# Reciprocals' transfers on ScalarE's queue, an earlier V, the last segment's skip in units 2 and 3, and a new rhythm of the convolution's lanes

## The chip, the core and the metric

The kernel runs on one core of a Trainium2 chip, as one program with one launch. The core has five engines with an instruction stream each: TensorE (PE, matmuls), VectorE (DVE), ScalarE (ACT), GpSimd (POOL) and SyncE (SP, which here does nothing but issue transfers). Transfers run on 16 DMA engines; SP, ACT and POOL can issue them, each on a queue of its own. The metric is the device time of one execution in microseconds, as the median of several runs.

## What is computed

A sequence of 2048 rows of 448 numbers goes through two branches, and a gate for each row mixes them. Branch A is a long convolution with a kernel that is itself computed from the parameters; branch B is attention in four segments of 512 rows with 16 heads of 28, causal inside a segment, plus a memory that later segments read from.

```python
# A: K = 2 Re sum_n C exp(A dt t); y = irfft(rfft(u) * rfft(K)); y + u * D_skip
# B, for each of the 4 segments s:
logits = einsum("bhqd,bhkd->bhqk", qs, ks) * scale + mask
a_dot = einsum("bhqk,bhkd->bhqd", softmax(logits), vs)
num, den = einsum("bhld,bhde->bhle", phi(qs), M), einsum("bhld,bhd->bhl", phi(qs), z) + 1e-6
o = g * num / den + (1 - g) * a_dot
M, z = M + phi(ks)^T vs, z + sum(phi(ks))
# out = gate * A + (1 - gate) * (o @ wo)
```

## The kernel before

The first half (up to about 430 us) builds the convolution's kernel, projects queries, keys and values and writes them to DRAM, and keeps the memory's part of each segment there too (`AM`, `DM`). The change lies in the second half, `second_half` (L1272).

Attention runs there in 16 **units**: unit `i` is one group of four heads (`hg = i % 4`) of segment `s = i // 4`. A unit has six **rounds**. In a round, `pair` (L1293) issues in turns the matmuls of the unit's logits (`weigh`, L1042: three parts into the PSUM bank `ps_w`, then ScalarE's Exp into `PT`) and the matmuls for the row maxima of the unit two ahead (`maxima`, L996: mask matmuls and products into the single bank `ps_mx`, then VectorE's reduction into `mx`). Behind that a round has one step each of other work, written as generators: in rounds 0 to 2 the weighted values of the unit before (`values`, L1074, into `ps_pv`, evicted to `pvs` by ScalarE), a step of the segment's end if one is open, and a step of the convolution. Matmuls keep their program order on TensorE (`k.mm`, L1463); what goes through `k.dve` and `k.sca` keeps it on VectorE and ScalarE (L1461). Transfers issued on SP may be reordered by the framework's planner when their data are ready earlier.

**The convolution** (`convolve`, L578) has 16 **lanes**, in units 1 to 12. A lane `m` is a transform T (`transform`, L610: eight matmuls on `gk` into the single bank `ps_c`, ScalarE's eviction to `ks`, and two transfers that swap the halves of `ks`), a product P (`product`, L618: eight matmuls on `gu` into `ps_c`, then two VectorE products with `ks` into `pr`, and the loads of a later lane), and a way back (`back`, L625) in two steps b and B of eight matmuls each into `ps_c`, with ScalarE's eviction to `bs` and a store to `BB` at the end. The loop (L645) gives one step at each `yield`: T of lane m, P of lane m - 1, then b and B of lane m - 2. The table `PACE` (L1402) says how many steps each round takes: 5.35 in a unit, so now and then a round has none.

**The end of a segment** (`seg_end`, L1190, opened in round 2 of units 4, 8 and 12) takes about 24 rounds. It loads four tiles `xt` of the input (`skip`, L1152), fetches the sums of the weights out of `pvs` into `dn` and the memory's sums into `dm`; `inverse` (L1097) takes reciprocals on VectorE, splits them into a high and a low part `rs` and sends both by transfer into the rows of `r8`, from where matmuls with `sel` spread them over the partitions. `norm` (L1131) does that for the softmax, `recall` (L1114) for the memory. Then follow the products with `wo` (`out_mm`), and `store` (L1165) adds the scaled `xt` and writes to `TB`. `scaled` (L1159) multiplies `xt` by the gate on ScalarE and by `D_skip` on GpSimd. All of these transfers go out on SP.

For the last segment the skip is done by itself (`skip_last`, L1171): four loads, four times `scaled`, four stores, in the last rounds of unit 10 and the first of unit 11; it shares the four `xt` buffers with `seg_end`. `values` asks for its segment's V (one buffer, 1 MB) at its first step, at the end of units 0, 4, 8 and 12.

Of the kernel before, what the change touches and what calls it, by code (L numbers as in the profile page):

```python
# [12 lines left out]
F32 = mybir.dt.float32  # L13
# [564 lines left out]
def convolve(nc, k, fp):  # L578

    NM = 16  # L580
    cf, cb, gk, gu, ks, pr = {}, {}, {}, {}, {}, {}
    rows = lambda t, m: t[4 * m : 4 * m + 4].rearrange("(i s) r n d -> (s r n) i d", i=2)
    halves = [slice(0, 64), slice(64, 128)]

    def load(m):
        if m >= NM:
            return
        if m % 2 == 0:
            cf[m // 2] = fp.tile([128, 4, 64], F32, tag="cf", name="cf", bufs=2)
            k.dma(cf[m // 2], k.c_fw[:, 2 * m : 2 * m + 4])  # L590
            cb[m // 2] = fp.tile([128, 2, 2, 2, 64], F32, tag="cb", name="cb", bufs=2)
            k.dma(cb[m // 2].rearrange("p m a s c -> p m (a s c)"), k.c_bk[:, m : m + 2])
        gk[m] = fp.tile([128, 2, D], F32, tag="gk", name="gk", bufs=2)
        k.dma(gk[m], rows(k.GK, m))
        gu[m] = fp.tile([128, 2, D], F32, tag="gu", name="gu", bufs=2)
        k.late(k.dma(gu[m], rows(k.GU, m)))

    def second(m, x):

        pt = k.ps("c")  # L600
        w = cf[m // 2]
        for s, r in enumerate(halves):
            for i, o in enumerate(halves):
                k.mm(
                    pt[o, s, :D], w[r, 2 * (m % 2) + i], x[r, i],
                    start=True, stop=True, tile_position=(64 * s, 64 * i),
                )
        return pt[:, :, :D]

    def transform(m):  # L610
        pt = second(m, gk.pop(m))
        ks[m] = fp.tile([128, 2, 2, D], F32, tag="ks", name="ks", bufs=2)
        k.sca.activation(ks[m][:, 0], pt, AF.Copy)
        x = ks[m].rearrange("(e a) b s d -> a e b s d", a=2)
        for a in range(2):
            k.dma(x[a, :, 1], x[1 - a, :, 0])

    def product(m):  # L618
        pt = second(m, gu.pop(m))
        pr[m] = fp.tile([128, 2, 2, D], F32, tag="pr", name="pr", bufs=2)  # L620
        x = ks.pop(m)
        for b in range(2):
            k.dve.tensor_tensor(pr[m][:, b], pt, x[:, b], ALU.mult)

    def back(m):  # L625

        pt = k.ps("c")
        w, x = cb[m // 2][:, m % 2], pr.pop(m)
        for b in range(2):
            if b:  # L630
                yield
            for i, r in enumerate(halves):
                for s, o in enumerate(halves):
                    k.mm(
                        pt[o, i, :D], w[r, b, s], x[r, b, s],
                        start=(b == 0), stop=(b == 1), tile_position=(64 * i, 64 * s),
                    )
        bs = fp.tile([128, 2, D], F32, tag="bs", name="bs", bufs=2)
        k.sca.activation(bs, pt[:, :, :D], AF.Copy)
        k.dma(k.BB[4 * m : 4 * m + 4].rearrange("(i s) r n d -> (s r n) i d", i=2), bs)  # L640

    load(0)
    load(1)
    yield
    for m in range(NM + 2):  # L645
        if m < NM:
            transform(m)
            yield
        if 1 <= m <= NM:
            product(m - 1)  # L650
            load(m + 1)
            yield
        if m >= 2:
            yield from back(m - 2)
            yield


def finish(nc, k, fp):
# [300 lines left out]
def attend(nc, k, ap):  # L959
# [82 lines left out]
    def weigh(i):  # L1042
# [23 lines left out]
        for hp in range(2):  # L1066
            for sl, pat in (
# [3 lines left out]
            ):  # L1071
                nc.gpsimd.affine_select(sl, sl, pat, ALU.is_ge, 0.0, base=0, channel_multiplier=-1)  # L1072

    def values(i):  # L1074
        s, hg = divmod(i, 4)
        if hg == 0:
            Vs[s] = ap.tile([128, 4, SEG], F32, tag="V", name="V", bufs=1)
            k.dma(Vs[s], k.VD[SEG * s : SEG * s + SEG].rearrange("(t p) h e -> p t (h e)", p=128))
            pvss[s] = ap.tile([128, 4, SEG], F32, tag="pvs", name="pvs", bufs=2)
        yield  # L1080
        V, pvs, PT = Vs[s], pvss[s], W.pop(i)
        pv = k.ps("pv")
        for kt in range(4):
            if kt in (1, 2):
                yield
            o = (0, 512, 1024, 896)[kt]
            for h in range(4):
                k.mm(
                    pv[32 * h : 32 * h + 32, 128 * kt :],
                    V[:, kt, (4 * hg + h) * 32 : (4 * hg + h) * 32 + 32],  # L1090
                    PT[:, h, o : o + SEG - 128 * kt],
                    start=(kt == 0), stop=(kt == 3), tile_position=(0, 32 * h),
                )
        act(pvs[:, hg], pv, AF.Copy)
        yield

    def inverse(x, rows, dst):  # L1097


        rc = ap.tile([128, 64], F32, tag="rc", name="rc", bufs=2)  # L1100
        rs = ap.tile([128, 2, 64], F32R, tag="rs", name="rs", bufs=2)
        v.reciprocal(rc, x)
        v.tensor_copy(rs[:, 0], rc)
        v.tensor_tensor(rs[:, 1], rc, rs[:, 0], ALU.subtract)
        for b in range(2):
            o = rows + 4 * b
            k.dma(
                dst[o : o + 4].rearrange("o h (i f) -> o (h i) f", f=64).bitcast(F32),
                rs[:, b].bitcast(F32),
            )  # L1110

    am, r8 = {}, {}

    def recall(s):  # L1114

        dn = ap.tile([128, 64], F32, tag="dm", name="dm", bufs=1)
        k.ldma(dn, k.DM[s - 1].rearrange("j h (i f) -> (j h i) f", f=64))
        yield
        v.tensor_scalar(dn, dn, 1e-6, None, ALU.add)
        inverse(dn, 32, r8[s - 1])  # L1120
        yield
        am[s] = ap.tile([128, 4, SEG], F32, tag="am", name="am", bufs=1)
        k.ldma(am[s], k.AM[:, :, s - 1].rearrange("h p q -> p h q"))
        yield
        for hg in range(4):
            pb = k.ps("m")
            k.mm(pb, k.sel[32:40], r8[s - 1][32:40, hg], start=True, stop=True)
            v.scalar_tensor_tensor(am[s][:, hg], am[s][:, hg], k.gh[:, hg : hg + 1], pb, ALU.mult, ALU.mult)
            yield

    def norm(s):  # L1131

        pvs = pvss[s]
        dn = ap.tile([128, 64], F32, tag="dn", name="dn", bufs=1)
        k.dma(
            dn,
            pvs.rearrange("(j e) h q -> e j (h q)", e=32)[28].rearrange("j (i f) -> j i f", f=64),
        )
        r8[s] = ap.tile([40, 4, SEG], F32R, tag="r8", name="r8", bufs=1)
        yield  # L1140
        inverse(dn, 0, r8[s])
        yield
        for hg in range(4):
            o = pvs[:, hg]
            pb = k.ps("m")
            k.mm(pb, k.sel[0:8], r8[s][0:8, hg], start=True, stop=True)
            v.scalar_tensor_tensor(o, o, k.omg[:, hg : hg + 1], pb, ALU.mult, ALU.mult)
            if s > 0:
                v.tensor_tensor(o, o, am[s][:, hg], ALU.add)
            yield  # L1150
# [39 lines left out]
    def seg_end(s):  # L1190
# [5 lines left out]
        yield  # L1196
        next(sums)
        yield
        for t in range(2):
            scaled(s, t, xts[t])  # L1200
        yield
# [1 line left out]
            scaled(s, t, xts[t])  # L1203
        next(memory)
        yield
        yield
        yield
        for _ in range(4):
# [55 lines left out]
                v.scalar_tensor_tensor(yd, po, k.ogt[:, i : i + 1], yd, ALU.mult, ALU.add)  # L1264
                (k.dma, k.adma)[t % 2](k.out[128 * i : 128 * i + 128], yd)

    k.load_wo = load_wo
    k.load, k.maxima, k.weigh, k.values, k.seg_end = load, maxima, weigh, values, seg_end
    k.half, k.divide, k.last_end, k.skip_last = half, divide, last_end, skip_last

# [1 line left out]
def second_half(nc, k, ap, tp, fp, fin):  # L1272
# [5 lines left out]
    def step(g):  # L1278
        return next(g, none) is not none
# [21 lines left out]
    def turn_over(n):  # L1301
        pt = k.ps("pv")
        for _ in range(n):
            k.mm(pt, wz[:, :128], wz, start=True, stop=True)
# [23 lines left out]
    fp = fp()  # L1328
    cv = convolve(nc, k, fp)
    step(cv)  # L1330
    vals = k.values(0)
    step(vals)
    for r in range(4):
        turn_over(3)
        peak(ms[1])
    ends, n, acc = [], 0, 0.0

    for i in range(16):
        if i > 0:
# [2 lines left out]
        behind = ms.get(i + 1, nothing)  # L1342
        w = k.weigh(i)
        for r in range(6):
            if i == 0:
                turn_over(3)
            pair(w, ahead)
            if r < 2:
                if r == 1 and k.half:
# [2 lines left out]
            if i > 0 and r < 3:  # L1352
                step(vals)
                if r == 2 and i % 4 == 0:
                    ends.append(k.seg_end(i // 4 - 1))
            for _ in range(2 if i > 13 or i == 13 and r > 1 else 1):
                if ends and not step(ends[0]):
# [3 lines left out]
                    step(ends[0])  # L1361
                k.divide(DIVIDE[i, r])
            if 1 <= i <= 12:
                acc += PACE[r]
                while acc >= 1.0:
                    acc -= 1.0
                    step(cv)
            if i == 10 and r == 2:
                skips = k.skip_last()
            if i == 10 and r > 2 or i == 11 and r < 3:  # L1370
                step(skips)
            if i == 13 and r < 5:
                load_b(r)
# [25 lines left out]
    k.last_end(vals)  # L1399


PACE = (0.9, 0.6, 0.8, 1.0, 1.0, 1.05)  # L1402
DIVIDE = {(14, 5): 0, (15, 2): 1, (15, 4): 2}


# [300 lines left out]
```

## Time and profile before

| | us |
|---|---|
| three runs | 818.84, 814.87, 810.97 |
| median | 814.87 |
| the profiled execution, its own time | 821.13 |
| its span on the core | 819.4 |

The profile shows one execution. Its page begins with the busy time of each engine, and cuts the span into 40 slices of 20.5 us; a digit is a tenth, 9 is 90% or more:

```profile
PE   1696998999979998799997789879996997978897
DVE  8879679878999689986886555557456753573386
ACT  4867789979998799987982145454344533351220
PEclk9998998999999999999998798998998789787899
DMA  9347774144541455513648779788569666464595
```

PEclk is the clock that TensorE was granted. The slices from the 24th to the 36th are units 0 to 12. A row of a timeline gives the start, the length, the engine, the line, the operation with its output and input and their shapes, how many there were, and in brackets how long the engine had been idle before and what ended that. In a row of waits stand the total, the number of waits and the longest. A row of a window gives the busy time of TensorE, its weight loads, VectorE, ScalarE and GpSimd, then the granted clock, the DMA share and GB/s.

### The profile page before, as it was taken

What the parts mean: (1) busy time and instruction counts of PE and PEld (TensorE: products, weight loads), DVE (VectorE), ACT (ScalarE), POOL (GpSimd) and SP (SyncE); (2) the same over time, 40 slices, a digit from 0 to 9 for tenths busy, and PEclk for the clock granted to TensorE, in tenths of its full rate; (3) what the DMA queues carried; (4) which work ended last, traced back from release to release, by engine and by line L of the source; (5) the groups of instructions that cost most, each with busy time, mean ns of one, the idle gap of its engine ahead of it and who ended that gap; (6) DMA issues with size and microseconds to landing.
All of it is one profiled execution on the core that took longest, in us unless ns stands there. A gap on an engine that the chain in (4) does not pass through costs nothing.

```text
span 819.4 us, 19938 instructions
## 1 busy us (share of the span) xinstructions
PE 702.9 (86%) x8343; PEld 380.8 (46%) x8343; DVE 578.8 (71%) x770; ACT 500.7 (61%) x611; POOL 156.6 (19%) x193
## 2 busy tenths in 40 slices
PE   1696998999979998799997789879996997978897
PEld 1363565766546655456654443333442333333433
DVE  8879679878999689986886555557456753573386
ACT  4867789979998799987982145454344533351220
POOL 6313210011101110011100021132112213140110
PEclk9998998999999999999998798998998789787899
DMA  9347774144541455513648779788569666464595
GB/s 253 99 110 237 230 230 136 36 151 155 188 161 58 133 172 169 167 61 116 209 176 294 300 273 275 265 278 272 192 211 308 198 210 224 155 237 167 135 293 180
DMA packets 91553, 158.03 MB, mean 193 GB/s; under 512 B 22175, under 2 KB 59543, under 8 KB 91463
## 3 DMA queue, kind: packets, MB, share of 16 engines
q1 hardware_dynamic: 87510, 154.04, 57.4%
q10 hardware_dynamic: 3072, 1.84, 0.8%
q8 instruction: 66, 1.08, 0.6%
q0 software_dynamic: 880, 0.87, 0.4%
q14 instruction: 25, 0.20, 0.1%
HBM read 88.51 MB, written 60.24 MB: 182 GB/s over the span
## 4 chain that ended last, share of the span: by engine, by line
PE 58%; ACT 14%; DVE 13%; DMA 8%; issue 4%; SPq 1%; ACTq 0%; POOL 0%; DVEq 0%
PE ps_m L1464 23%; PE ps_c L1464 8%; PE ps_w L1464 6%; PE ps_arg L1464 6%; ACT cs L1418 5%; PE ps_pv L1464 5%; PE ps_mx L1464 5%; PE ps_k L1464 5%; DVE mx L1418 2%; DVE Y L404 2%; PE ps_m L1467 2%; ACT PT L1418 2%; DMA dn<-pvs 1%; DVE cs L384 1%; DMA ks<-ks 1%
## 5 line engine op out<-in xcount | busy, mean ns | idle before, releaser
L1418 ACT ACTIVATE PT<-ps_w 128x1024 f32<-128x1024 f32 (+1 forms) x96 | 84.5, 880 | 157.6 <-PE ps_w L1464 155.1
L1418 DVE TENSOR_REDUCE mx<-ps_mx 128x2 f32<-128x1024 f32 (+3 forms) x128 | 102.4, 821 | 86.0 <-PE ps_mx L1464 82.4
L361 POOL TENSOR_TENSOR EX<-EX,cab 128x1024 f32<-128x1024 f32 x28 | 53.5, 1912 | 299.0 <-ACT EX L1418 252.4
L1418 ACT ACTIVATE cs<-ps_arg 128x1024 f32<-128x1024 f32 x97 | 94.5, 1023 | 13.1 <-DVE cs L384 10.8
L1464 PE MATMUL ps_w<-qu,ku 32*128 32x512 f32 (+3 forms) x768 | 96.5, 368 | 4.5 <-ACT PT L1418 3.4
L1464 PEld LDWEIGHTS ps_w<-qu,ku 32*128 32x128 f32 x768 | 63.5, 201 | 76.5 <-issue 36.5
L1072 POOL TENSOR_SCALAR_AFFINE_SELECT PT<-PT 128x256 f32<-128x256 f32 (+1 forms) x96 | 46.5, 485 | 245.0 <-ACT PT L1418 245.0
L1464 PE MATMUL ps_m<-xh,w 112*128 112x512 f32 x256 | 91.5, 410 | 1.4 <-DMA w<-WD 1.4
L1464 PE MATMUL ps_k<-Y,X 128*32 128x64 f32 x3584 | 63.1, 223 | 14.6 <-DVE Y L405 14.5
L400 DVE TENSOR_TENSOR X<-EX,cs 128x1024 f32<-128x1024 f32 x56 | 70.2, 1254 | 7.5 <-ACT cs L1418 7.0
L1464 PEld LDWEIGHTS ps_k<-Y,X 128*32 128x32 f32 x3584 | 53.9, 112 | 40.3 <-DVE Y L405 26.2
L404 DVE TENSOR_TENSOR Y<-EY,cs 128x1024 f32<-128x1024 f32 x56 | 69.1, 1235 | 0.0
L1418 ACT ACTIVATE cs<-cs,bhp 128x1024 f32<-128x1024 f32 x56 | 64.3, 1149 | 1.4
L1464 PEld LDWEIGHTS ps_m<-xh,w 112*128 112x128 f32 x256 | 48.0, 188 | 20.3 <-issue 7.4
L1418 ACT ACTIVATE EY<-ps_arg 128x1024 f32<-128x1024 f32 x52 | 52.6, 1033 | 6.7 <-PE ps_arg L1464 6.4
L1464 PE MATMUL ps_m<-wo,pvs 128*128 128x448 f32 x96 | 46.4, 611 | 7.6 <-ACT mn L1418 4.6
L1464 PE MATMUL ps_pv<-PT,V 128*32 128x128 f32 (+3 forms) x512 | 51.0, 499 | 0.0
L406 DVE SCALAR_TENSOR_TENSOR Y<-EY,cs 128x512 f32<-128x512 f32 x56 | 40.0, 714 | 15.3 <-ACT cs L1418 14.2
L1464 PE MATMUL ps_m<-xl,w 112*128 112x512 f32 x128 | 50.2, 392 | 0.0
L1464 PE MATMUL ps_c<-pr,cb 64*64 64x448 f32 x256 | 36.6, 645 | 15.2 <-DVE pr L1418 13.7
L1464 PE MATMUL ps_mx<-ku,qu 32*128 32x512 f32 (+3 forms) x256 | 47.4, 403 | 0.0
L1464 PE MATMUL ps_arg<-ct,lh 64*128 64x512 bf16 x224 | 44.0, 382 | 3.8 <-ACT cs L1418 2.8
(217 smaller groups left out, 1313.6 us busy)
## 6 DMA issues: line engine op xcount, KB each, us to landing
w<-WD SPq DMA_DIRECT2D x32, 448.0 KB
qu<-QD SPq DMA_DIRECT2D x16, 512.0 KB
ku<-KD SPq DMA_DIRECT2D x16, 512.0 KB
GU<-gs SPq DMA_DIRECT2D x32, 224.0 KB
GK<-gs SPq DMA_DIRECT2D x8, 896.0 KB
gk<-GK SPq DMA_DIRECT2D x16, 448.0 KB
gu<-GU SPq DMA_DIRECT2D x16, 448.0 KB
ks<-ks SPq DMA_DIRECT2D x32, 224.0 KB
```

What stands on the lines that cost most here:

```text
L361: nc.gpsimd.tensor_tensor(o, o, cab, ALU.mult)
L384: v.tensor_scalar(t[:, 0].rearrange("p w t c -> p t w c").bitcast(I32), pv.bitcast(I32), 0x7FFFFFFF, None, ALU.bitwise_and)
L400: v.tensor_tensor(X, ex, t[:, :, 0], ALU.mult)
L404: v.tensor_tensor(Y[:, :, :, :32], lo, y[:, :, :, ::-1], ALU.mult)
L406: v.scalar_tensor_tensor(Y[:, 1, :, 32:], ey[:, :, 32:], -1.0, y[:, 1], ALU.mult, ALU.mult)
L1072: nc.gpsimd.affine_select(sl, sl, pat, ALU.is_ge, 0.0, base=0, channel_multiplier=-1)
L1418: x = op(*args, **kw)
L1464: tc.keep_in_program_order(nc.tensor.matmul(*args, **kw))
L1467: tc.keep_in_program_order(nc.tensor.transpose(*args))
```

## The change

- **Transfers of the reciprocals.** `inverse` gets a `yield` between the reciprocals and the two transfers, and these and the fetch of `dn` go out on ScalarE's queue, pinned to their place in its program order. `seg_end` makes the extra steps in rounds that it had already, so that its length stays.
- **V.** Its load moves out of `values` into `load_v`, called in round 2 of units 4, 8 and 12 ahead of the segment's end, and for the first segment before unit 0.
- **The last segment's skip.** `skip_last` is stepped in rounds 0, 4 and 5 of unit 2 and 0, 1 and 2 of unit 3.
- **The lanes.** `PACE` goes. Each round of units 1 to 12 takes one step; a lane's steps are T, P of the lane before, an empty one, and then b and B of that same lane, so that the way back comes two rounds behind its product. After B of every second lane the generator yields true, and the round takes the next step (the next T) as well. `pr` has one buffer in place of two.
- **Unit 13.** In rounds 3 and 4 two filling matmuls each (`turn_over`, L1301) go ahead of the round's pair.

```diff
     def product(m):
-        pr[m] = fp.tile([128, 2, 2, D], F32, tag="pr", name="pr", bufs=2)
+        pr[m] = fp.tile([128, 2, 2, D], F32, tag="pr", name="pr", bufs=1)
...
-    for m in range(NM + 2):
+    for m in range(NM + 1):
         if m < NM:
             transform(m)
             yield
-        if 1 <= m <= NM:
+        if m >= 1:
             product(m - 1)
             load(m + 1)
             yield
-        if m >= 2:
-            yield from back(m - 2)
             yield
+            yield from back(m - 1)
+            yield m % 2 == 0
...
+    def load_v(s):
+        Vs[s] = ap.tile([128, 4, SEG], F32, tag="V", name="V", bufs=1)
+        k.dma(Vs[s], k.VD[SEG * s : SEG * s + SEG].rearrange("(t p) h e -> p t (h e)", p=128))
+
     def values(i):
         if hg == 0:
-            Vs[s] = ap.tile([128, 4, SEG], F32, tag="V", name="V", bufs=1)
-            k.dma(Vs[s], k.VD[SEG * s : SEG * s + SEG].rearrange("(t p) h e -> p t (h e)", p=128))
...
     def inverse(x, rows, dst):
         v.tensor_tensor(rs[:, 1], rc, rs[:, 0], ALU.subtract)
+        yield
         for b in range(2):
             o = rows + 4 * b
-            k.dma(
+            k.pin(k.adma(
                 dst[o : o + 4].rearrange("o h (i f) -> o (h i) f", f=64).bitcast(F32),
                 rs[:, b].bitcast(F32),
-            )
+            ))
...
-        inverse(dn, 32, r8[s - 1])
+        yield from inverse(dn, 32, r8[s - 1])
...
-        k.dma(
+        k.pin(k.adma(
             dn,
             pvs.rearrange("(j e) h q -> e j (h q)", e=32)[28].rearrange("j (i f) -> j i f", f=64),
-        )
+        ))
...
-        inverse(dn, 0, r8[s])
+        yield from inverse(dn, 0, r8[s])
...
         next(sums)
         yield
+        next(sums)
         for t in range(2):
             scaled(s, t, xts[t])
...
         next(memory)
         yield
+        next(memory)
         yield
...
+    skips = k.skip_last()
     for i in range(16):
         for r in range(6):
-            if i == 0:
-                turn_over(3)
+            if i == 0 or i == 13 and r in (3, 4):
+                turn_over(3 if i == 0 else 2)
             pair(w, ahead)
...
                 if r == 2 and i % 4 == 0:
+                    k.load_v(i // 4)
                     ends.append(k.seg_end(i // 4 - 1))
...
             if 1 <= i <= 12:
-                acc += PACE[r]
-                while acc >= 1.0:
-                    acc -= 1.0
+                if next(cv, False):
                     step(cv)
-            if i == 10 and r == 2:
-                skips = k.skip_last()
-            if i == 10 and r > 2 or i == 11 and r < 3:
+            if (i, r) in SKIPS:
                 step(skips)
...
-PACE = (0.9, 0.6, 0.8, 1.0, 1.0, 1.05)
+SKIPS = ((2, 0), (2, 4), (2, 5), (3, 0), (3, 1), (3, 2))
```

More of the change, by code (lines that the diff above doesn't have):

```diff
@@ L1265, in last_end @@
                 (k.dma, k.adma)[t % 2](k.out[128 * i : 128 * i + 128], yd)
-    k.load_wo = load_wo
+    k.load_wo, k.load_v = load_wo, load_v
     k.load, k.maxima, k.weigh, k.values, k.seg_end = load, maxima, weigh, values, seg_end
@@ L1330, in second_half @@
     step(cv)
+    k.load_v(0)
     vals = k.values(0)
@@ L1335, in second_half @@
         peak(ms[1])
-    ends, n, acc = [], 0, 0.0
+    ends, n = [], 0
+    skips = k.skip_last()
     for i in range(16):
```

## The prediction

> **What bounds the kernel now.** I read the page first, then who waited for whom on TensorE in the stage that the change touches, then the timelines at its waits, then the granted clock there. The page:
>
> ```profile
> span 819.4 us, 19938 instructions
> PE 702.9 (86%) x8343; PEld 380.8 (46%) x8343; DVE 578.8 (71%) x770; ACT 500.7 (61%) x611; POOL 156.6 (19%) x193
> ```
>
> TensorE is busy for 86% of the span and runs its matmuls in program order, so time is won where it stands still or runs slowly. The profiled execution took 821.13 us, 0.8% above the median of 814.87 (810.97 to 818.84); I sum against 821.13 and carry the difference over. All edits but one lie between 490 and 742 us (units 1 to 12):
>
> ```profile
> 490.00:742.00 252.00, 217.66 (x2417) 91.19 (x2410) 147.54 (x190) 110.62 (x149) 61.70 (x105) 0.86 0.71 237
> PE ps_c L1464 <- DVE pr L1418: 13.7, 7, 6.0
> PE ps_m L1464 <- ACT mn L1418: 4.6, 2, 4.4
> PE ps_mx L1464 <- DVE mx L1418: 4.4, 2, 2.9
> PE ps_c L1464 <- issue: 2.9, 2, 1.6
> ```
>
> 34 of these 252 us are idle and the mean clock is 0.86. The four waits hold 25.6 us. Where the clock was low (second-last but one number of each row):
>
> ```profile
> 498.00:507.00 9.00, 8.87 (x80) 2.96 (x75) 4.30 (x6) 2.51 (x3) 1.04 (x2) 0.62 0.88 289
> 519.00:522.00 3.00, 3.00 (x18) 0.51 (x16) 1.23 (x1) 1.02 (x1) 0.41 (x1) 0.50 0.87 344
> 552.00:558.00 6.00, 5.04 (x46) 1.48 (x45) 5.90 (x9) 2.13 (x3) 2.55 (x3) 0.72 0.65 189
> 570.00:579.00 9.00, 8.88 (x53) 2.79 (x48) 3.20 (x3) 3.11 (x4) 1.39 (x3) 0.62 0.86 309
> 633.00:639.00 6.00, 6.00 (x40) 1.46 (x36) 3.37 (x6) 2.14 (x3) 1.54 (x3) 0.54 0.72 258
> 648.00:663.00 15.00, 14.88 (x109) 5.04 (x108) 10.88 (x15) 5.17 (x7) 1.92 (x4) 0.54 0.63 203
> 690.00:693.00 3.00, 3.00 (x4) 0.94 (x4) 0.00 (x0) 0.00 (x0) 0.77 (x2) 0.50 0.30 92
> 702.00:714.00 12.00, 10.34 (x79) 3.37 (x73) 6.24 (x7) 3.07 (x4) 1.04 (x2) 0.57 0.43 150
> ```
>
> Lost clock is (1 - clock) x length: 3.4, 1.5, 1.7, 3.4, 2.8, 6.9, 1.5 and 5.2 us. Each stretch stands just behind a wait of 1.3 us or more, so a wait costs its length and then some clock, as the second of these two did, while the first left the clock at full:
>
> ```profile
> 530.69 0.98 PE L1464 MATMUL ps_c<-pr,cb 64*64 64x448 f32 x8 [1.37 <-DVE pr L1418]
> ...
> 568.70 0.98 PE L1464 MATMUL ps_c<-pr,cb 64*64 64x448 f32 x8 [1.67 <-DVE pr L1418]
> ```
>
> **Reciprocals' transfers on ScalarE's queue.** At two segment ends VectorE stood at the reciprocal until `dn` had landed, and TensorE stood behind VectorE:
>
> ```profile
> 541.17 0.86 PE L1464 MATMUL ps_pv<-PT,V 128*32 128x256 f32 x16
> 543.31 0.38 SPq L1480 DMA_DIRECT2D V<-VD  x1
> 543.94 0.63 SPq L1480 DMA_DIRECT2D dn<-pvs  x1
> ...
> 550.91 0.55 DVE L1418 RECIPROCAL rc<-dn 128x64 f32<-128x64 f32 x1 [3.79 <-DMA dn<-pvs]
> 552.96 0.23 PE L1464 MATMUL ps_mx<-mk 32*128 32x128 bf16 x2 [2.88 <-DVE mx L1418]
> ...
> 632.75 1.02 PE L1464 MATMUL ps_c<-pr,cb 64*64 64x448 f32 x4 [5.98 <-DVE pr L1418]
> 543.94 6.95 DMA dn<-pvs
> qu<-mn POOLq DMA_DIRECT2D x16, 8.0 KB, 3.6
> L235 ACTq DMA_DIRECT2D SP<-sp x6: 557/558/667, 33.2 to 52.1; - x6
> ```
>
> `dn` (32 KB) was asked for behind V (1 MB) and took 6.95 us. The nearest small transfer off SP's queue landed in 3.6 us, which is 3.35 less; VectorE waited 3.79. I take 3.6 (small, another queue, the same stage): the wait is nearly gone, and the ends are all of it or nothing. Gain: 2.88 + 5.98 = 8.9 us idle and the clock behind them, 1.7 + 2.8 = 4.5 us. What is late next is the product behind the reciprocals, so in the second end it also matters that no product shares the reciprocals' round any more. Cost: five issues for each segment end, 0.56 us each on ACT, two of them in the round in which ACT also has two `xt` scalings and, at the first end, the `bs` eviction: 1 us, between 0 (hidden beside ACT's idle half) and 3 x 1.1 (each pair on the path). Behind a pair that waits for VectorE stands the next PT, but the added yield puts it a round after `rs` is written. The Trainium skill (DMA: Bandwidth & Descriptors, Issuing engines are not separate DMA queues) speaks against the gain: issuing from several engines saves only the issuing time. No row here has a small transfer on ACT's queue beside V; by that rule the sum would be 13.4 us longer.
>
> **V asked for sooner** changes nothing: V already went out 1.3 us after the last matmul that reads the old V (541.17 + 0.86), before its program place. **`pr` with one buffer** costs nothing: it is written again a lane after its reader.
>
> **Last segment's skip in units 2 and 3.** In unit 10 these four tiles waited for buffers still in use, and ACT, in order, held back all behind them:
>
> ```profile
> 679.03 4.32 DMA TB<-xt
> 683.41 4.50 DMA xt<-in_A_u
> 687.99 0.67 ACT L1418 ACTIVATE xt<-xt,gt 128x448 f32<-128x448 f32 x1 [6.95 <-DMA xt<-in_A_u]
> 689.77 1.11 PE L1464 MATMUL ps_m<-wo,pvs 128*128 128x448 f32 x1 [4.37 <-ACT mn L1418]
> ```
>
> Gain: 4.4 us and the clock's 1.5. The same loads, scalings, POOL products and stores move to 506 to 530 us, where all four buffers are free and the loads have four rounds (some 14 us, a round being 252 / 72); 4 x 0.67 us of ACT lies in rounds in which ACT has room. Cost 0; if the loads were late, at most the same 4.4.
>
> **The lanes' new rhythm.** Before, a lane made four steps in about 4.5 rounds: T (transform), P (product), then b and B (the two halves of a way back). Now it is T, P, an empty round, b, B, and after every second B the next T in the same round: again 4.5. A lane before (with its P, then b):
>
> ```profile
> 514.10 0.98 PE L1464 MATMUL ps_c<-gu,cf 64*64 64x448 f32 x8 [0.36 <-ACT ks L1418]
> ...
> 515.22 2.09 DVE L1418 TENSOR_TENSOR pr<-ps_c,ks 128x896 f32<-128x896 f32 x2 [0.83 <-PE ps_c L1464]
> 515.24 0.39 PE L1464 MATMUL ps_w<-qu,ku 32*128 32x256 f32 x4
> 515.67 0.60 ACT L1418 ACTIVATE PT<-ps_w 128x512 f32<-128x512 f32 x1 [1.14 <-PE ps_w L1464]
> 517.23 0.68 DVE L1418 TENSOR_REDUCE mx<-ps_mx 128x2 f32<-128x512 f32 x1
> 517.46 0.98 PE L1464 MATMUL ps_c<-pr,cb 64*64 64x448 f32 x8 [1.83 <-DVE pr L1418]
> ```
>
> b waits 1.83 us for `pr`. But VectorE then still owes the round's maxima until 517.91, and the next round's mask matmuls need their bank. Before, b's 0.98 us covered that. In an empty round TensorE ends at 515.63, waits for PT until 516.3, does 0.2 us and waits for the maxima until 517.9: 2.1 us in two pieces. The wait goes from `ps_c` to `ps_mx` and grows. By my count of rounds five lanes have next to nothing else there (2.1 each), eight have values or output matmuls of some 0.9 us (1.3 each), three have both (0.8 each): 23.3 us. About 27% of the stage runs at half clock (2 x 34.5 / 252), where matmuls leave no wait: 17. Before it was 13.7 - 6.0 + 1.3 (the second "issue" wait) = 9.0. Added: 8 us; the ends are -9 (nothing moves) and +14 (all at full clock).
>
> B and T together, seven times: T needs the bank that ACT is still evicting.
>
> ```profile
> 544.53 0.98 PE L1464 MATMUL ps_c<-pr,cb 64*64 64x448 f32 x8
> 545.63 0.92 ACT L1418 ACTIVATE bs<-ps_c 128x896 f32<-128x896 f32 x1
> 546.60 0.98 PE L1464 MATMUL ps_c<-gk,cf 64*64 64x448 f32 x8 [0.21 <-ACT bs L1418]
> ```
>
> B ended at 545.51, the bank was free at 546.60: 1.09 x 7 = 7.6 us. Between came other matmuls before; now nothing does. The clock behind the lanes' waits cost 1.5 + 3.4 + 6.9 + 5.2 = 17.0 us for five waits of 1.3 to 1.8 (the one of 1.37 cost none); I count seven such, 24: added 7. One wait goes: the third T comes two rounds later, so its `gk` has landed (1.59 us of "issue", and 3.4 of clock behind it): gain 5.0.
>
> **Filling matmuls in unit 13.** Their like, in the groups by form (mean of one in ns behind the busy time):
>
> ```profile
> L1464 PE MATMUL ps_pv<-wz 128*128 128x512 bf16 x30 | 10.1, 454 | 0.0
> ```
>
> Four are at most 1.8 us, in rounds in which TensorE waits anyway: 0.5.
>
> **Sum.** Gains 8.9 + 4.5 + 5.9 + 5.0 = 24.3. Costs 8 + 7.6 + 7 + 1 + 0.5 = 24.1. So 821 stays 821, and the median about 815.
>
> **Rivals.** Faster: short waits cost no clock. Then the lanes' 17 us of clock go as well as the 7 that I added, and at full clock their waits are 6 longer: 815 - 17 - 7 + 6 = 797. For it speaks that the longest new piece is about 1.3 us and one of 1.37 left the clock at full; against it, 1.67 us at 568.7 was followed by 0.62. It decides from a limit of about 1.4 us. The Trainium skill (TensorE: Matmul & The Clock Gate, HAM oscillation) has a far higher limit: only gaps above some 3.4 us throttle; the waits of 1.3 to 1.8 us here do not agree. Slower: the waits behind B cost clock too: seven at 3.4 us (17.0 / 5), half of it inside stretches that are slow already, 12 more: 827; it decides once 1.1 us is enough. Slower too, and the change not doing what it says: `dn` lands no sooner on its new queue, and 13.4 come back: 828.
>
> **How the numbers follow.** As summed 0.37 (own range 806 to 824), short waits free 0.33, B's waits dear 0.22, `dn` no sooner 0.08. About 1% (8.1 us) is what a measurement of this kernel tells from no change. Faster by more: 0.33 x 0.9 and a little of the first, 0.33; slower: 0.22 x 0.9, 0.08 x 0.8 and a little, 0.29; same 0.38. Range: 794 (the 797 and its scatter) to 831.
>
> **What would show it.** No VectorE wait above 1 us for `dn`; no ACT wait for `xt` in unit 10; TensorE's wait for `pr` near 0 and its wait for `mx` up from 4.4 to over 12; seven waits of 1.1 us for `bs`. Wrong if `mx` waits do not grow, if the clock between 490 and 742 leaves 0.86 by more than 0.03, or if SP's order puts something new ahead of `ks` or `gk`.

## The result and the profile after

The changed kernel takes 826.5 us, the median of 13 runs (817.54 to 836.83). In the same session the kernel before took 814.87 (13 runs, 810.97 to 822.57). The ratio is 1.0104, with a 95% interval of 1.0063 to 1.0146: slower by about 1%, 8.5 us. (Ratios here leave out runs over 1.5% slower than the kernel's fastest, four of these 13, so this one is nearer to 1 than that of the two medians.) The forecast was 815 in a range of 794 to 831; the time lies inside the range and on the side of the rivals that were slower.

The profiled execution of the changed kernel took 831.22 us, 0.6% above its median, at a mean granted clock of 0.911. That is the lowest of its 13 runs (median 0.935, highest 0.951), so its rows are read below for waits, and the clock is taken from all runs. First its page, the span and the busy times of the engines:

```profile
span 829.5 us, 19917 instructions
PE 708.0 (85%) x8339; PEld 380.1 (46%) x8347; DVE 576.7 (70%) x770; ACT 502.1 (61%) x611; POOL 156.3 (19%) x193
```

The work is the same to a few instructions. To compare the stage, the cut is made at the same points of the program, the third and the fifteenth issue of `qu` from `mn` on GpSimd, which the timelines give at 490.50 and 729.97 us before and at 488.59 and 738.99 after. The windows view between them (length, then the busy time of TensorE first, the granted clock last but two), of the kernel before:

```profile
490.50:729.97 239.47, 209.22 (x2332) 85.74 (x2329) 138.12 (x177) 107.30 (x144) 59.25 (x101) 0.88 0.70 230
```

and of the kernel after:

```profile
488.59:738.99 250.40, 215.97 (x2324) 87.50 (x2321) 136.32 (x177) 107.57 (x143) 59.46 (x100) 0.86 0.65 218
```

The stretch is 10.9 us longer, about as much as the two profiles differ (10.1). TensorE's idle time in it (the length less its busy time) went from 30.3 to 34.4 us, and the rest, 6.8 us, is the same matmuls at a lower clock. How much of these 6.8 us is due to the change, two profiles can't tell: with V moved alone, an experiment below that changed no time, the profile has 205.09 us of matmuls between the same two points, 4.1 less than before, and the same idle time of 30.2. What TensorE waited for, in the waits view of the kernel after from 490 to 752 us (total, times, longest):

```profile
PE ps_mx L1468 <- DVE mx L1422: 17.6, 16, 2.5
PE ps_c L1468 <- ACT bs L1422: 7.8, 8, 1.1
PE ps_w L1468 <- ACT PT L1422: 6.7, 13, 1.1
PE ps_m L1468 <- DVE pvs L1422: 2.5, 2, 1.5
...
PE ps_m L1468 <- ACT mn L1422: 0.5, 2, 0.3
```

The wait for `pr` (13.7 before) has gone altogether and the one for `mn` (4.6) nearly. In their place stand many short waits: for `mx` 17.6 in place of 4.4, for `bs` 7.8 in place of 1.0, for PT 6.7 in place of 1.4. How a lane makes them is seen in the timeline of the kernel after, at the first segment's end:

```profile
543.57 2.09 DVE L1422 TENSOR_TENSOR pr<-ps_c,ks 128x896 f32<-128x896 f32 x2 [0.74 <-ACT pvs L1422]
...
545.57 0.39 PE L1468 MATMUL ps_w<-qu,ku 32*128 32x256 f32 x2 [1.12 <-ACT PT L1422]
...
545.57 1.28 DVE L1422 TENSOR_REDUCE mx<-ps_mx 128x2 f32<-128x768 f32 x2
...
546.90 0.23 PE L1468 MATMUL ps_mx<-mk 32*128 32x128 bf16 x2 [0.95 <-DVE mx L1422]
...
547.37 0.98 PE L1468 MATMUL ps_c<-pr,cb 64*64 64x448 f32 x8
```

VectorE makes `pr` for 2.09 us and only then the maxima. In the empty round TensorE first waits 1.12 us for ScalarE's PT, does 0.4 us of logits and waits 0.95 us for the maxima's bank. When b comes, two rounds behind its product, `pr` is ready, and b has no wait of VectorE's left to cover.

Another part of the change, the transfer of `dn`, is in the chain of waits (start, length) of the kernel after:

```profile
543.32 7.66 DMA dn<-pvs
...
638.21 8.69 DMA dn<-pvs
```

On ScalarE's queue, with nothing ahead of it there, it took 7.66 and 8.69 us, longer than the 6.95 and 4.88 at the same two segment ends before. VectorE's wait for it did not fall either:

```profile
DVE rc L1422 <- DMA dn<-pvs: 8.4, 2, 5.6
```

It was 7.3 before. Yet TensorE stood less behind it, as its timeline at the second segment's end shows:

```profile
646.93 0.55 DVE L1422 RECIPROCAL rc<-dn 128x64 f32<-128x64 f32 x1 [5.59 <-DMA dn<-pvs]
...
648.62 0.29 PE L1468 MATMUL ps_mx<-mk 32*128 32x128 bf16 x2 [1.60 <-DVE mx L1422]
```

VectorE stood 5.59 us here and TensorE 1.60, where TensorE stood 5.98 before: no product waits in the reciprocals' round any more. At the first end TensorE waited 2.46 us for `mx`, where it was 2.88.

### The profile page after: what moved, and what is told of

The parts are those of the page before. It is cut to its first block, busy times and chain, and to the rows that moved or that the text cites. A ratio compares the mean times of both kernels' runs of the same rounds, so it can differ in the third digit from the quotient of the medians.

```text
span 829.5 us, 19917 instructions
## 1 busy us (share of the span) xinstructions
PE 708.0 (85%) x8339; PEld 380.1 (46%) x8347; DVE 576.7 (70%) x770; ACT 502.1 (61%) x611; POOL 156.3 (19%) x193
## 4 chain that ended last, share of the span: by engine, by line
PE 59%; DVE 17%; ACT 13%; DMA 5%; issue 5%; SPq 1%; DVEq 0%; ACTq 0%
PE ps_m L1468 23%; PE ps_c L1468 8%; PE ps_arg L1468 6%; PE ps_w L1468 5%; PE ps_pv L1468 5%; ACT cs L1422 5%; PE ps_mx L1468 5%; PE ps_k L1468 5%; DVE mx L1422 3%; DMA dn<-pvs 2%; DVE Y L404 2%; DVE pr L1422 2%; DVE cs L384 1%; PE ps_m L1471 1%; DVE Y L405 1%
## 5 line engine op out<-in xcount | busy, mean ns | idle before, releaser
L1468 PE MATMUL ps_w<-qu,ku 32*128 32x512 f32 (+3 forms) x768 | 101.5, 378 | 9.1 <-ACT PT L1422 8.4
L1422 ACT ACTIVATE cs<-ps_arg 128x1024 f32<-128x1024 f32 x97 | 94.6, 1024 | 13.3 <-DVE cs L384 10.9
L1468 PE MATMUL ps_mx<-mk 32*128 32x128 bf16 (+5 forms) x768 | 38.4, 223 | 23.5 <-DVE mx L1422 23.5
L406 DVE SCALAR_TENSOR_TENSOR Y<-EY,cs 128x512 f32<-128x512 f32 x56 | 40.0, 714 | 15.3 <-ACT cs L1422 14.2
L1468 PE MATMUL ps_mx<-ku,qu 32*128 32x512 f32 (+3 forms) x256 | 49.3, 417 | 0.0
```

The source lines that it names most:

```text
L406: v.scalar_tensor_tensor(Y[:, 1, :, 32:], ey[:, :, 32:], -1.0, y[:, 1], ALU.mult, ALU.mult)
L1422: x = op(*args, **kw)
L1468: tc.keep_in_program_order(nc.tensor.matmul(*args, **kw))
```

## The experiments

All ratios are to the kernel before on the same chip, with 95% intervals; a hundredth is 8.2 us.

### The lanes' rhythm alone

The kernel before, with the new order of the steps and `pr` in one buffer.

```diff
-    for m in range(NM + 2):
+    for m in range(NM + 1):
...
-        if m >= 2:
-            yield from back(m - 2)
             yield
+            yield from back(m - 1)
+            yield m % 2 == 0
...
-                acc += PACE[r]
-                while acc >= 1.0:
-                    acc -= 1.0
+                if next(cv, False):
                     step(cv)
```

> The kernel before with the lanes' new rhythm alone (and pr in one buffer). Theory (the rhythm is what costs): 10 to 17 us slower; TensorE's waits for mx between units 1 and 12 rise from 4.4 us to 15 or more, those for bs from 1.0 to about 8, those for pr fall from 13.7 to near 0. Rival (the transfers on ScalarE's queue hold ScalarE and cost it): within 3 us of before, and the waits for mx grow less than the waits for pr fall.

The ratio was 1.0135 [1.0091, 1.0180], 11 us slower. The windows view between the same two points of the program:

```profile
488.99:740.56 251.57, 211.96 (x2324) 86.33 (x2321) 139.44 (x177) 107.29 (x143) 59.42 (x101) 0.88 0.67 218
```

Against the kernel before the stretch is 12.1 us longer, of which 9.4 are idle (39.6 for 30.3) and 2.7 matmul time. The mean clock of the run is no lower: over all runs of the two its median is 0.937 here and 0.931 before. Its waits:

```profile
PE ps_mx L1462 <- DVE mx L1416: 19.8, 16, 2.9
PE ps_w L1462 <- ACT PT L1416: 9.8, 14, 3.1
PE ps_c L1462 <- ACT bs L1416: 7.4, 7, 1.1
```

So the rhythm by itself makes the new waits and more than the whole loss, and here it costs mostly as idle time. Single places do lose clock: in the unit that begins at 601.99 us before and 607.58 here, TensorE was at full clock before,

```profile
608.70:619.90 11.20, 10.42 (x137) 4.09 (x136) 9.59 (x12) 5.99 (x8) 2.49 (x5) 1.00 0.80 252
```

and here, behind a wait of 1.12 us for PT and one of 0.96 for `mx` 1.3 us later, the last part of the unit ran at 0.67 on average, with no idle time:

```profile
622.00:633.20 11.20, 11.20 (x99) 3.61 (x91) 4.55 (x5) 4.58 (x6) 1.46 (x3) 0.67 0.48 166
```

In the changed kernel the same pair of waits stands at the same place, and the 12 us behind it ran at 0.50. The Trainium skill (TensorE: Matmul & The Clock Gate, HAM oscillation) asks for no idle gaps above some 3.4 us; two pieces that are 2.1 us together stay within that rule, and the clock fell all the same.

### The last segment's skip alone

The kernel before, with `skip_last` stepped at the new places.

```diff
-            if i == 10 and r == 2:
-                skips = k.skip_last()
-            if i == 10 and r > 2 or i == 11 and r < 3:
+            if (i, r) in SKIPS:
                 step(skips)
```

> The kernel before with the last segment's skip in units 2 and 3 alone. Theory: the 4.4 us wait in unit 10 and 1.5 us of clock go, nothing new comes: 6 us faster. Rival (the loads and stores in units 2 and 3 get in the way of the lanes' own transfers): 0 or slower, with new waits for ks or gk between 500 and 540 us.

The ratio was 0.9928 [0.9896, 0.9960], 5.9 us faster. TensorE's wait for `mn` fell from 4.6 to 0.6 us, and ScalarE's longest wait for an `xt` fell from 6.9 to 2.7 us:

```profile
ACT xt L1418 <- DMA xt<-in_A_u: 2.7, 1, 2.7
```

### The transfers alone, and their extra step alone

First the kernel before with `dn` and the two `rs` on ScalarE's queue and the added `yield`; then the same with the `yield` only, and all transfers on SP.

```diff
         v.tensor_tensor(rs[:, 1], rc, rs[:, 0], ALU.subtract)
+        yield
         for b in range(2):
             o = rows + 4 * b
-            k.dma(
+            k.pin(k.adma(
```

> The kernel before with the fetch of dn and the reciprocals' transfers on ScalarE's queue alone. Prediction as given: dn lands in about 3.6 us, VectorE's wait for it goes, 13 us faster. Theory from the changed kernel's chain (dn took 7.66 and 8.69 us on its new queue): dn lands no sooner than the 6.95 and 4.88 us of before, within 4 us of before. Rival (ScalarE held by its own transfers): 6 us slower or more, with ACT idle in front of xt.

> The kernel before with the extra step between the reciprocals and their transfers alone, all transfers on SP. Theory (what the transfers' part gained, 4.7 us, comes from SP no longer standing still for rs, 15.3 us in the trace of before, in front of other transfers): within 3 us of before, SP's wait for rs stays at 10 us or more. Rival (it is the step, which gives VectorE's results time): the same 4 to 5 us faster as with ScalarE's queue.

With the queue the ratio was 0.9943 [0.9903, 0.9984], 4.7 us faster; with the step alone 1.0047 [1.0020, 1.0074], 3.8 us slower. So the queue brings a gain (some 8 us against the step alone, in another session), but not by the way that was forecast. The chain of waits of the kernel with both has `dn` at

```profile
541.38 7.01 DMA dn<-pvs
...
622.67 7.03 DMA dn<-pvs
...
713.78 5.18 DMA dn<-pvs
```

which is no sooner than on SP's queue (6.73, 5.89 and 5.08 us with the step alone), and VectorE still waits for it, 6.7 us in place of 7.3. The idle time between the two points of the program did not fall either: 31.3 us (235.82 less 204.51) for 30.3.

```profile
491.40:727.22 235.82, 204.51 (x2356) 85.12 (x2356) 137.04 (x178) 107.35 (x144) 59.48 (x100) 0.91 0.71 234
```

What is shorter in this profile is the time of the same matmuls, by 4.7 us; by itself that proves little, since it is 4.1 us shorter with V alone, too. But the clock points the same way: its median over the runs is 0.942 here, 0.931 in the kernel before and 0.933 with the step alone. What did go is SP's own wait for the reciprocals, 15.3 us before and unchanged with the step alone (the DMA queue's waits, step alone):

```profile
SPq L1483 <- DVE rs L1421: 15.8, 5, 5.3
```

Whether the gain comes from the freer SP, and how that would leave TensorE a higher clock, these runs do not settle.

### Everything but the rhythm

The changed kernel with the old loop, `PACE` and two `pr` buffers.

```diff
-            yield
-            yield from back(m - 1)
-            yield m % 2 == 0
+        if m >= 2:
+            yield from back(m - 2)
+            yield
```

> The changed kernel with the lanes' old rhythm (PACE, way back of the lane before, pr in two buffers). Theory (the rhythm costs, the skip gains, the transfers are about even): 4 to 8 us faster than before, some 14 faster than the changed kernel. Rival (the transfers cost): no faster than before.

The ratio was 0.9850 [0.9809, 0.9891], 12.3 us faster than before; the medians, 808.39 and 819.49 us, give 0.986. Against the whole change (1.0104) the rhythm is therefore worth 2.6%, some 21 us, in this company, and 11 alone. Between the two points of the program:

```profile
494.30:726.30 232.00, 205.34 (x2328) 85.03 (x2324) 137.02 (x177) 107.35 (x144) 59.56 (x100) 0.90 0.71 238
```

TensorE is idle for 26.7 us of it, 7.8 less than in the whole change; that is the smaller part of the 21. The clock's median over the runs is 0.945 here and 0.935 in the whole change, so much of the rest may be clock that the rhythm takes away in this company and not alone; that was not taken apart further. TensorE's wait for `pr` is back:

```profile
PE ps_c L1471 <- DVE pr L1425: 12.8, 7, 4.3
```

### V alone

The kernel before with `load_v` and its two calls.

```diff
+    def load_v(s):
+        Vs[s] = ap.tile([128, 4, SEG], F32, tag="V", name="V", bufs=1)
...
                 if r == 2 and i % 4 == 0:
+                    k.load_v(i // 4)
```

> The kernel before with V's load at its new place in the program alone. Theory (the planner had it out already, right behind the last matmul on the old V): V goes out within 1.5 us of that matmul as before, the same time within 2 us. Rival (the earlier place puts V ahead of something that mattered): over 3 us slower.

The ratio was 1.0007 [0.9974, 1.0039]: no difference.

### The empty round elsewhere, and half of it away

Two variants of the changed kernel. In the first the empty step stands between T and P. In the second only every second lane has one, and B and T never share a round.

```diff
         if m >= 1:
+            yield
             product(m - 1)
             load(m + 1)
             yield
-            yield
             yield from back(m - 1)
```

> The changed kernel with the empty step between T and P in place of between P and b: as many empty rounds, and B and T together as often. Theory (what costs is that nothing covers VectorE's debt behind P): waits for mx fall from 17.6 us to about 5, waits for pr come back (7 to 13), waits for bs stay at 7 to 8, 4 to 8 us faster than the changed kernel. Rival (any empty round costs the same, since then nothing covers the wait for PT): waits for PT rise by what those for mx lose, time as the changed kernel's within 3 us.

```diff
             load(m + 1)
             yield
-            yield
+            if m % 2:
+                yield
             yield from back(m - 1)
-            yield m % 2 == 0
+            yield
```

> The changed kernel with an empty step behind P in every second lane only, and no round with B and T together; again 4.5 rounds a lane. Theory (empty rounds and B with T both cost): waits for bs fall from 7.8 to 1 or 2, waits for mx by about half to 9, waits for pr of 3 to 6 come, 8 to 12 us faster than the changed kernel, some 816 where before has 815. Rival (the B with T rounds cost next to nothing, since what is saved there is waited for elsewhere): within 4 us of the changed kernel.

The first came to 1.0009 [0.9967, 1.0050], 8 us better than the whole change. Its waits:

```profile
PE ps_w L1468 <- ACT PT L1422: 9.5, 13, 1.6
PE ps_c L1468 <- DVE pr L1422: 9.3, 7, 2.9
PE ps_c L1468 <- ACT bs L1422: 7.3, 7, 1.1
...
PE ps_mx L1468 <- DVE mx L1422: 2.7, 3, 2.2
```

The wait for the maxima fell from 17.6 to 2.7 as soon as b stood right behind P again, and the wait for `pr` came back: the two are one debt of VectorE, paid at one place or at the other. But the 8 us are not seen as idle time. Between the two points of the program this kernel has

```profile
499.57:742.50 242.93, 207.63 (x2330) 85.97 (x2327) 137.09 (x177) 107.19 (x143) 59.44 (x101) 0.89 0.69 226
```

that is 35.3 us idle, no less than the 34.4 of the whole change: what `mx` gave back, `pr`, PT and some waits that the profile puts down to no releaser took. The median clock is higher, 0.943 for 0.935. Why the place that the change chose is the dearer one therefore stays open. The second came to 0.9928 [0.9890, 0.9966], 14 us better than the whole change:

```profile
PE ps_mx L1469 <- DVE mx L1423: 10.4, 9, 4.3
PE ps_c L1469 <- DVE pr L1423: 7.7, 6, 2.3
...
PE ps_c L1469 <- ACT bs L1423: 1.1, 3, 0.5
```

The waits for `bs` are nearly gone (1.1 for 7.8), as no round has B and T together any more, and those for `mx` are about half. Which of the two brings the 14 us, this run can't tell.

### `dn` ahead of V, and `xt` in three orders

These stand on the kernel with everything but the rhythm. First, `dn` back on SP, with V and `xt` issued behind it:

```diff
-        k.pin(k.adma(
+        k.first = k.dma(
             dn,
...
+        with k.issue_after(k.first) if s > 0 else ExitStack():
             k.dma(Vs[s], k.VD[SEG * s : SEG * s + SEG].rearrange("(t p) h e -> p t (h e)", p=128))
...
+        with k.issue_after(k.first) if s < 3 else ExitStack():
             k.ldma(xt, k.u[128 * i : 128 * i + 128])
```

> The changed kernel with the old rhythm, the fetch of dn back on SP's queue, and V and the four xt of a segment's end issued behind it there (in the other kernels V and at two of the three ends xt go out ahead of it). Theory (dn lands late because the transfers ahead of it, V above all, fill the 16 DMA engines, whatever its queue): dn lands in 3 to 4 us, VectorE's wait for it falls from 7.1 us to under 1, and the kernel is 5 to 9 us faster than with V ahead, that is 800 to 805 us where before has 815. Rival (the fetch is slow by itself, 128 pieces of 256 bytes out of four partitions): it lands in 5 us or more again and the time is that of the old rhythm with V ahead, some 808. V may then be late for its first use, which would show as a wait of TensorE before ps_pv in units 5, 9 and 13.

The ratio was 0.9857 [0.9820, 0.9894], the same as without. VectorE's wait for `dn` is gone from its list: `dn` has landed before VectorE asks for it, 4.2 us after its issue at the latest, on the old queue and by order of issue alone. But `xt` is now late, and ScalarE, in order, stands at its scaling:

```profile
ACT xt L1427 <- DMA ks<-ks: 5.8, 1, 5.8
ACT xt L1427 <- DMA BB<-bs: 5.6, 1, 5.6
ACT xt L1427 <- DMA xt<-in_A_u: 3.0, 3, 1.6
```

(The first two name what landed last by the profile; what the scaling reads is `xt`.) TensorE's wait for PT, which ScalarE makes behind it, went from 3.8 to 8.1 us. The two ways out of that: `dn`, then `xt`, then V; and `xt` asked for two rounds sooner, in round 0 of units 4, 8 and 12, where its buffers are free.

```diff
-        load_v(s + 1)
         xts = [skip(s, t) for t in range(4)]
+        load_v(s + 1)
```

```diff
+            if r == 0 and i in (4, 8, 12):
+                k.early_skip(i // 4 - 1)
```

> As dn_first, with the order dn, xt, V in place of dn, V, xt. Theory (each waits for what stands ahead of it): ScalarE's waits for xt fall to 2 to 5 us, V lands 2 to 3 us later and is still in time for its first use; between dn_first and xt_early, 2 to 6 us faster than dn_first. Rival (V then is the last and late): a wait of TensorE of 1 us or more before the first ps_pv of units 5, 9 or 13, and no gain.

> As dn_first, and the four xt of a segment's end asked for two rounds sooner, in round 0 of units 4, 8 and 12, so that only V comes behind dn. In dn_first VectorE no longer waits for dn, but ScalarE waits 14.4 us for xt (before: 8.0), which land behind V. Theory (the wait only moved to what is next behind V): ScalarE's waits for xt at the segment ends fall under 2 us, VectorE's for dn stay near 0, 4 to 8 us faster than dn_first, some 800 where before has 815. Rival (ScalarE's wait at xt costs nothing): within 3 us of dn_first.

With V last the ratio was 0.9938 [0.9906, 0.9970], worse by 7 us than with `dn` first: the values now wait for V, 10.4 us in place of at most 0.9 in the other kernels, and ScalarE's wait at `xt` did not go.

```profile
PE ps_pv L1475 <- DMA V<-VD: 10.4, 3, 4.8
...
ACT xt L1429 <- DMA ks<-ks: 16.5, 2, 8.7
```

With `xt` early it was 0.9804 [0.9763, 0.9845] (798.65 us), 4 us better than `dn` first; the intervals overlap, so that a gain over it is not shown. Its waits at `dn` and `xt` did not go as the step meant:

```profile
DVE rc L1435 <- DMA dn<-pvs: 4.8, 2, 3.1
...
ACT xt L1435 <- DVE dm L1435: 6.2, 1, 6.2
ACT xt L1435 <- DMA BB<-bs: 4.5, 1, 4.5
```

and `dn` took 6.82 us again, though it went out ahead of V:

```profile
538.45 6.82 DMA dn<-pvs
```

So V is not the only traffic that counts. Here the loads `gk` and `gu`, 448 KB each, had been issued 3.1 and 1.3 us ahead of `dn`, in the kernel with `dn` first the nearest one 2.5 us ahead; that fits, but was not tried by itself. Where the gain of this version lies, if there is one, is open, too. Its median clock, 0.955, is the highest of all.

### Without the filling matmuls

Everything but the rhythm, less the filling matmuls of unit 13.

```diff
-            if i == 0 or i == 13 and r in (3, 4):
-                turn_over(3 if i == 0 else 2)
+            if i == 0:
+                turn_over(3)
```

> The changed kernel with the old rhythm and without the four filling matmuls of unit 13. Theory of the prediction (0.5 us of cost, in rounds in which TensorE waits anyway): within 2 us of the same kernel with them. Rival (they keep the clock up there): 3 us slower or more, with a lower clock between units 13 and 14.

The ratio was 0.9814 [0.9764, 0.9865] (802.89 us) against 0.9850 [0.9809, 0.9891] with them. The intervals overlap: the filling is worth nothing to some 3 us of loss, and no gain is to be seen. This version and the one with `xt` early are the best of the study; the two together were not tried.

## Why the prediction was off

| part | forecast, us | measured alone, us (95%) |
|---|---|---|
| transfers on ScalarE's queue | -12.4 | -4.7 (-7.9 to -1.3) |
| V | 0 | +0.6 (-2.1 to +3.2) |
| last segment's skip | -5.9 | -5.9 (-8.5 to -3.3) |
| rhythm | +17.6 | +11 (+7.5 to +14.7), in the whole change +21 |
| filling | +0.5 | between 0 and +3, unclear |

The time lies inside the range and near one of the rivals, but in part by luck: the sum missed in two places, the transfers and the rhythm. The parts measured alone add up to about 1 us, with some 6 us either way by their intervals, and the whole change took 8.5, so it is not clear that they simply add.

**The step that failed** is "The nearest small transfer off SP's queue landed in 3.6 us ... I take 3.6". `dn` on ScalarE's queue took 7.0 us in the experiment and 7.66 and 8.69 in the changed kernel. The row that it was taken from, `qu` from `mn`, is 8 KB at other moments; `dn` is 32 KB and goes out beside V, 0.3 to 1.2 us behind it. At the second segment end even 3.6 us would not have done: `dn` took 4.88 there before and VectorE waited 3.04 for it, so landing in 3.6 saves 1.3, while TensorE's whole wait of 5.98 was booked as a gain. The rule that the prediction set against it, of the Trainium skill (DMA: Bandwidth & Descriptors, Issuing engines are not separate DMA queues), held for the landing: the queue of the issuer did not bring it forward. The rival "`dn` lands no sooner" had 828 us and a chance of 0.08; its condition came true and the time is 826.5. Its chance was too low: a row of another size at another time outweighed a rule that spoke of this very case. That its time fits so well is luck, though: it put the parts other than the rhythm at -4.4 us, and they measured -12.3, while the rhythm came to 21 for its 17.6.

The rival's price of 13.4 us was not exact either. TensorE's two waits behind `dn` went from 8.9 to 4.1 us (2.46 and 1.60) without a sooner landing, most of it at the second end, where "no product shares the reciprocals' round any more", and the transfers brought 4.7 us of their own, which came with a higher clock and not with shorter waits.

**The rhythm** made the waits that were described. The pieces, 17 us by the forecast, are the waits for `mx` less the two behind `dn` (17.6 - 4.1 = 13.5) and the growth of those for PT (6.7 - 1.4 = 5.3): 18.8. The waits for `bs`, 7.6 by the forecast, are 7.8, and the two waits of `ps_c` on "issue" (2.9), one of them for `gk`, are gone. What was uncertain is the clock: "I count seven such, 24: added 7". Alone, the rhythm left the run's mean clock where it was (0.937 for 0.931; TensorE's matmuls took 2.7 us more), and its price was 11 us, 7 less than forecast; in the whole change it was 21 against a forecast of 17.6, with only 7.8 of it as idle time. So the 8.5 us by which the sum was too low divide into the parts other than the rhythm (forecast -17.8, measured -12.3) and the rhythm in their company (3 us more, within the interval).

**The skip** met its price of 5.9 us, with 2.6 either way by its interval, and **V** cost nothing, as forecast. **`pr`** with one buffer was run only together with the rhythm. **The filling** at 0.5 us is not decided by its run.

**The rivals of the clock.** "Short waits cost no clock" (797) did not come: in the unit shown, clock was lost behind a lane's pair of waits, and the median time is on the other side. But one half of it, that the rhythm adds no lost clock, is near to what the rhythm alone showed. "B's waits dear" (827) ended near the time, but its mechanism is not what the runs show: the version with few waits for `mx`, but with all seven waits for `bs`, had a median clock of 0.943, above the kernel before (0.931) and like that of the version without the waits for `bs` (0.941).

Of the signs that were named beforehand: TensorE's wait for `pr` near 0, that for `mx` over 12, seven waits of 1.1 us for `bs` all came, and the clock between 490 and 742 us stayed at 0.86 in the profile. "No VectorE wait above 1 us for `dn`" did not come true (5.6), and pointed at the failed step at once. ScalarE's wait for `xt` in the last segment's skip went, but two others took its place at the segments' ends, one of them, by the profile, for `r` (the waits of ScalarE after):

```profile
ACT xt L1422 <- DMA r<-rs: 4.8, 2, 4.0
ACT xt L1422 <- DMA qu<-QD: 3.7, 1, 3.7
```

## What to carry to other kernels

- When a consumer is moved away from its producer, look at what else the producer's engine still owes in order. Here VectorE's maxima stood behind the product; b right behind P waited visibly, but covered them; with b taken away, TensorE waited for the maxima (17.6 us for 4.4). Which place is cheaper has to be measured: the idle time was nearly the same (35.3 and 34.4 us), and the runs were 8 us apart.
- Another issuing queue did not bring this small transfer forward beside a large one. What brought `dn` in before it was needed was issuing the large ones behind it, and then the next in line (`xt`, V) became the wait, so that no time was won. What gave a clean gain (5.9 us) was moving a set of loads as a whole to where its buffers are free, as with the skip of the last segment.
- Price a transfer by a row of its own size beside the same traffic, and give a rule that says "no gain" more than 0.08 when no such row exists.

## What the runs showed of the hardware

- A 32 KB transfer took 5.0 to 8.7 us where it went out on ScalarE's queue 0.3 to 1.6 us behind a 1 MB one on SP's, and 4.8 to 7.3 us where both went out on SP's. With the half of the empty rounds away it once went out on ScalarE's queue 0.3 us ahead of the 1 MB, and VectorE had it without a wait 4.8 us later. On SP's queue 0.7 us ahead of it, it had landed after 4.2 us at the latest in the kernel with `dn` first, but took 6.82 us once in the one with `xt` early.
- Two waits of 1.12 and 0.96 us within 2.5 us were followed by 11 to 12 us of a mean granted clock of 0.67 and 0.50 (two kernels) while TensorE was never idle, where the same unit without them ran at 1.00.
- With a few issues moved from SP's to ScalarE's queue TensorE's idle time in the stage stayed (31.3 for 30.3 us), and the median of the runs' mean clock was 0.942 in place of 0.931. Why is open.
